# A gated linear attention kernel: per-head vector work gathered into operations over all heads, and the loop over heads put in another order

## The chip, the cores and the metric

One core of a Trainium2 chip. The metric is the device time of one execution in microseconds (us), taken as the median of several runs. The engines are TensorE (PE, whose weight loads the profile calls PEld), VectorE (DVE), ScalarE (ACT), GpSimd (POOL) and SyncE (SP), which issues the DMAs here. All data is float32 unless said otherwise.

## The reference

Two stages stand one behind the other. The first is a gated linear attention with a complex decay, over 4 batches, 8 heads, 768 steps and a head dimension of 48; the second sends each of the 3072 rows of 384 numbers through the one expert of eight that its gate picks.

```python
mag = sqrt(a_re**2 + a_im**2); scale = minimum(mag, 0.999) / (mag + 1e-6)
a = (a_re + 1j * a_im) * scale                     # one factor per batch, head, step and row of the state
for t in range(768):
    S = a[:, :, t, :, None] * S                    # state 48 x 48 per batch and head
    S.re += einsum('bhd,bhe->bhde', k[:, :, t], v[:, :, t])
    y[:, :, t] = einsum('bhd,bhde->bhe', q[:, :, t], S.re)
x = y.transpose(0, 2, 1, 3).reshape(3072, 384)
...                                                # gate: logits, argmax, softmax weight
out[mask] = gate_w[mask, None] * (maximum(x[mask] @ w1[e], 0) @ w2[e])   # for each expert e
```

## The kernel before, in words

The attention runs in six chunks (loop over `c`) of L = 128 steps, for all BH = 32 pairs of batch and head together. The states `S0r` and `S0i` stay in SBUF from chunk to chunk. A chunk has four parts:

- **Loads** (`load_t`, lines 159 to 166). v comes in four DMAs. a_re and a_im come pair by pair: a DMA into `raw` (two buffers), a transpose on PE into a PSUM tile `tp`, and a copy on DVE into `are` or `aim`, which hold 48 partitions x 4096 elements.
- **Scan** (lines 173 to 211). DVE scales the factors and forms running complex products over the 128 steps in seven doubling steps, on whole 48 x 4096 tiles. The result is `cr` and `ci`. `qc` and `kc` serve as scratch, and after seven swaps `are` and `aim` are free.
- **Loads of q and k** (lines 212 and 213) into `qc` and `kc`, by the same `load_t`.
- **Loop over the 32 heads** (lines 215 to 290). With c the running product, DVE forms Q = q c (`Qr`, `Qi`) and K = k c / |c|^2 (`Kr`, `Ki`, by way of `m2`, `t3` and a reciprocal, line 232). PE multiplies them to the 128 x 128 scores `Wt` (lines 240 and 241), DVE copies these out of PSUM, and POOL sets those above the diagonal to zero (`affine_select`, line 244). PE forms y from the scores and v and from Q and the state (lines 246, 247 and 250); DVE copies y; PE transposes it (254); DVE copies again and SP stores it into `x_attn` in DRAM. Then K is transposed (260, 264), multiplied with v (`Pr`, `Pi`, lines 268 and 270), and ten small operations on DVE (279 to 290) make the new state of the head.

All PSUM tiles of the attention (`tp`, `Wt_ps`, `y_ps`, `yT_ps`, `KrT_ps`, `KiT_ps`, `Pr_ps`, `Pi_ps`) share one tag `"r"` with four buffers. Tiles in SBUF from `pool` have two buffers, those from `big` one.

The tile framework puts in all the waits, hands out the buffers, and plans the order in which each engine gets its instructions, from the order of the source and an estimate of when each instruction can run. So the order on an engine is not always that of the source. Each engine then works through its own list in order.

The expert part (`moe_bf16`, lines 18 to 102) starts with a DMA of the whole `x_attn` into `xT` (line 32). It is not part of the change.

Of the kernel before, what the change touches and what calls it, by code (L numbers as in the profile page):

```python
# [10 lines left out]
F32 = mybir.dt.float32  # L11
BF16 = mybir.dt.bfloat16
AX = mybir.AxisListType
Alu = mybir.AluOpType
# [91 lines left out]
def kernel(  # L106
# [14 lines left out]
    nc = tc.nc  # L121
    B, H, S, D = q.shape
    BH = B * H
    L = 128
# [12 lines left out]
    ppool = ctx.enter_context(tc.psum_pool(name="ps", bufs=2))  # L137
# [4 lines left out]
    ident = cpool.tile([128, 128], F32, name="ident")  # L142
# [8 lines left out]
    for c in range(NC):  # L151
# [59 lines left out]
        cr, ci = cs, ci_s  # L211
        load_t(qc, q)
        load_t(kc, k)

        for bh in range(BH):
            b = bh // H
            h = bh % H
            crb = cr[:, b, h, :]
            cib = ci[:, b, h, :]
            qb = qc[:, b, h, :]  # L220
            kb = kc[:, b, h, :]
            vb = vc[:, b, h, :]
            Qr = pool.tile([D, L], F32, name="Qr")
            Qi = pool.tile([D, L], F32, name="Qi")
            nc.vector.tensor_tensor(Qr[:], qb, crb, Alu.mult)
            nc.vector.tensor_tensor(Qi[:], qb, cib, Alu.mult)
            m2 = pool.tile([D, L], F32, name="m2")
            t3 = pool.tile([D, L], F32, name="t3")
            nc.vector.tensor_tensor(m2[:], crb, crb, Alu.mult)
            nc.vector.tensor_tensor(t3[:], cib, cib, Alu.mult)  # L230
            nc.vector.tensor_tensor(m2[:], m2[:], t3[:], Alu.add)
            nc.vector.reciprocal(m2[:], m2[:])  # L232
            Kr = pool.tile([D, L], F32, name="Kr")
            Ki = pool.tile([D, L], F32, name="Ki")
            nc.vector.tensor_tensor(Kr[:], kb, crb, Alu.mult)
            nc.vector.tensor_tensor(Kr[:], Kr[:], m2[:], Alu.mult)  # L236
            nc.vector.tensor_tensor(Ki[:], kb, cib, Alu.mult)
            nc.vector.tensor_tensor(Ki[:], Ki[:], m2[:], Alu.mult)  # L238
            Wt_ps = ppool.tile([L, L], F32, name="Wt_ps", tag="r", bufs=4)
            nc.tensor.matmul(Wt_ps[:], Kr[:], Qr[:], start=True, stop=False)  # L240
            nc.tensor.matmul(Wt_ps[:], Ki[:], Qi[:], start=False, stop=True)  # L241
# [3 lines left out]
            y_ps = ppool.tile([L, D], F32, name="y_ps", tag="r", bufs=4)  # L245
            nc.tensor.matmul(y_ps[:], Wt[:], vb, start=True, stop=False)  # L246
            nc.tensor.matmul(y_ps[:], Qr[:], S0r[bh][:], start=False, stop=False)  # L247
# [143 lines left out]
```

## Time and profile before

| what | value |
|---|---|
| time, median of 4 runs | 4247.18 us (4245.32 to 4248.85) |
| the profiled execution | 4248.85 us, its span 4247.1 us |
| busy share of the span | PE 39%, PEld 23%, DVE 72%, ACT 1%, POOL 2% |
| granted TensorE clock | 1.000 |
| instructions on DVE | 7480 |
| chain that ended last, by engine | DVE 47%, PE 31%, DMA 15%, issue 4%, POOL 2%, ACT 1% |

The busy share is a mean over the span; the six chunks and the expert part behind them have different limits. The chain is followed back from the last instruction, at each step to what released it. The first chunk's scan ends at 299 us, its q and k loads at 367 us, its heads at 613 us; the last chunk's heads end at 3649 us.

### The profile page before, as it was taken

What the parts mean: (1) busy time and instruction counts of PE and PEld (TensorE: products, weight loads), DVE (VectorE), ACT (ScalarE), POOL (GpSimd) and SP (SyncE); (2) the same over time, 40 slices, a digit from 0 to 9 for tenths busy, and PEclk for the clock granted to TensorE, in tenths of its full rate; (3) what the DMA queues carried; (4) which work ended last, traced back from release to release, by engine and by line L of the source; (5) the groups of instructions that cost most, each with busy time, mean ns of one, the idle gap of its engine ahead of it and who ended that gap; (6) DMA issues with size and microseconds to landing.
All of it is one profiled execution on the core that took longest, in us unless ns stands there. A gap on an engine that the chain in (4) does not pass through costs nothing.

```text
span 4247.1 us, 25082 instructions
## 1 busy us (share of the span) xinstructions
PE 1676.0 (39%) x6864; PEld 971.9 (23%) x6864; DVE 3067.5 (72%) x7480; ACT 29.1 (1%) x32; POOL 83.0 (2%) x199
## 2 busy tenths in 40 slices
PE   2005541015540025530045520055410155599999
PEld 0003430003420014310024300034200043444444
DVE  4995756976748957749957659867579667777776
ACT  0000000000000000000000000000000000000000
POOL 0000000000000000000000000000000000000000
PEclk9999999999999999999999999999999999999999
DMA  1000000000010000010000000000000000401001
GB/s 24 0 4 13 4 15 12 0 10 8 3 20 6 0 14 4 4 24 0 0 16 4 12 15 0 7 10 3 17 9 0 13 5 4 165 30 60 30 1 45
DMA packets 167213, 64.62 MB, mean 15 GB/s; under 512 B 143138, under 2 KB 163618, under 8 KB 166690
## 3 DMA queue, kind: packets, MB, share of 16 engines
q1 hardware_dynamic: 167074, 63.02, 6.0%
q8 instruction: 56, 0.92, 0.1%
q14 instruction: 83, 0.68, 0.1%
HBM read 53.51 MB, written 9.44 MB: 15 GB/s over the span
## 4 chain that ended last, share of the span: by engine, by line
DVE 47%; PE 31%; DMA 15%; issue 4%; POOL 2%; ACT 1%; SPq 0%; DVEq 0%; POOLq 0%; ACTq 0%
PE z_ps L97 6%; PE hT_ps L93 5%; DMA raw<-in_a_re_dram 4%; DMA raw<-in_a_im_dram 4%; DVE qc L203 4%; DVE kc L204 4%; DVE kc L201 4%; DVE qc L200 4%; DVE cr L185 4%; DVE m L232 4%; PE tp L165 3%; DMA raw<-in_k_dram 3%; PE Wt_ps L240 3%; PE y_ps L246 3%; DMA raw<-in_q_dram 3%
## 5 line engine op out<-in xcount | busy, mean ns | idle before, releaser
L165 PE MATMUL tp<-ident,raw 128*48 128x128 f32 x768 | 288.4, 381 | 1894.5 <-DVE qc L166 1300.3
L165 PEld LDWEIGHTS tp<-ident,raw 128*48 128x48 f32 x768 | 88.2, 116 | 2093.4 <-DVE qc L166 1402.9
L95 DVE TENSOR_SCALAR hT<-hT_ps 128x512 bf16<-128x512 f32 x384 | 254.4, 689 | 137.5 <-PE hT_ps L93 120.2
L97 PE MATMUL z_ps<-w2e,hT 128*128 128x384 bf16 x1536 | 287.5, 328 | 9.2 <-DVE hT L95 7.6
L240 PE MATMUL Wt_ps<-Qr,Kr 48*128 48x128 f32 x384 | 152.0, 498 | 347.1 <-DVE Kr L236 347.1
L93 PE MATMUL hT_ps<-xTb,w1e 128*128 128x512 bf16 x1152 | 285.5, 381 | 0.1
L252 DVE COPY y_sb<-y_ps 128x48 f32<-128x48 f32 x192 | 39.9, 208 | 266.4 <-PE y_ps L250 265.5
L246 PE MATMUL y_ps<-vc,Wt 128*128 128x48 f32 x384 | 126.8, 430 | 183.1 <-POOL Wt L244 183.1
L166 DVE COPY are<-tp 48x128 f32<-48x128 f32 x192 | 53.8, 283 | 177.7 <-PE tp L165 176.8
L240 PEld LDWEIGHTS Wt_ps<-Qr,Kr 48*128 48x128 f32 x384 | 95.5, 307 | 377.1 <-DVE Kr L236 374.1
L232 DVE RECIPROCAL m<-m 48x128 f32<-48x128 f32 x192 | 179.3, 934 | 0.2
L97 PEld LDWEIGHTS <-hT 128*128 128x128 bf16 x1536 | 123.4, 97 | 176.8 <-DVE hT L95 122.7
L185 DVE RECIPROCAL cr<-cr 48x4096 f32<-48x4096 f32 x6 | 154.5, 25745 | 0.2
L166 DVE COPY aim<-tp 48x128 f32<-48x128 f32 x192 | 52.5, 282 | 138.2 <-PE tp L165 137.2
L244 POOL TENSOR_SCALAR_AFFINE_SELECT Wt<-Wt 128x128 f32<-128x128 f32 x192 | 82.0, 427 | 3547.4 <-DVE Wt L243 3547.4
L166 DVE COPY kc<-tp 48x128 f32<-48x128 f32 x192 | 52.9, 278 | 136.2 <-PE tp L165 135.7
L246 PEld LDWEIGHTS y_ps<-vc,Wt 128*128 128x128 f32 x384 | 95.9, 310 | 239.6 <-POOL Wt L244 239.6
L241 PE MATMUL Wt_ps<-Qi,Ki 48*128 48x128 f32 x384 | 140.7, 469 | 5.8 <-DVE Ki L238 5.8
L93 PEld LDWEIGHTS <-w1e 128*128 128x128 bf16 x1152 | 113.3, 98 | 118.1 <-issue 2.1
L166 DVE COPY qc<-tp 48x128 f32<-48x128 f32 x192 | 50.5, 277 | 108.4 <-PE tp L165 108.1
L247 PE MATMUL y_ps<-S0rA,Qr 48*128 48x48 f32 x384 | 126.8, 428 | 0.0
L250 PE MATMUL y_ps<-S0iA,negQi 48*128 48x48 f32 x384 | 119.7, 410 | 0.0
(2005 smaller groups left out, 3551.1 us busy)
## 6 DMA issues: line engine op xcount, KB each, us to landing
w1f<-in_moe_w_dram SPq DMA_DIRECT2D x8, 1536.0 KB, 6.5
w2f<-in_moe_w_dram SPq DMA_DIRECT2D x8, 1536.0 KB, 8.0
vc<-in_v_dram SPq DMA_DIRECT2D x24, 192.0 KB, 3.8
raw<-in_a_re_dram SPq DMA_DIRECT2D x192, 24.0 KB, 1.7
raw<-in_a_im_dram SPq DMA_DIRECT2D x192, 24.0 KB, 1.7
raw<-in_q_dram SPq DMA_DIRECT2D x192, 24.0 KB, 1.7
raw<-in_k_dram SPq DMA_DIRECT2D x192, 24.0 KB, 1.7
x_attn<-yT_sb SPq DMA_DIRECT2D x192, 24.0 KB, 1.4
```

The lines of the kernel that those rows point to most:

```text
L93: nc.tensor.matmul(hT_ps[:], w1e[:, dc, fc * 128:(fc + 1) * 128], xTb[:, dc, t0:t0 + TTK], start=(dc == 0), stop=(dc == nDC - 1))
L95: nc.vector.tensor_relu(hT[:], hT_ps[:])
L97: nc.tensor.matmul(z_ps[z][:], hT[:, z * nT:(z + 1) * nT], w2e[:, fc, :], start=(fc == 0), stop=(fc == nF - 1))
L165: nc.tensor.transpose(tp[:], raw[:], ident[:L, :L])
L166: nc.vector.tensor_copy(dst[:, b_, h_, :], tp[:])
L185: nc.vector.reciprocal(tmp[:], tmp[:])
L200: nc.vector.tensor_tensor(tA[:, :, :, :n_], a_hi, a_lo, Alu.mult)
L201: nc.vector.tensor_tensor(tB[:, :, :, :n_], b_hi, b_lo, Alu.mult)
L203: nc.vector.tensor_tensor(tA[:, :, :, :n_], a_hi, b_lo, Alu.mult)
L232: nc.vector.reciprocal(m2[:], m2[:])
L240: nc.tensor.matmul(Wt_ps[:], Kr[:], Qr[:], start=True, stop=False)
L246: nc.tensor.matmul(y_ps[:], Wt[:], vb, start=True, stop=False)
```

## The change

Per-head operations on DVE become operations over all heads. Q (`arf`, `aif`, in place of `are` and `aim`), the squared magnitude and its reciprocal (`m2a`, the reciprocal in 16 slices of 256 elements), and minus the imaginary part of Q (`t3a`) are formed once per chunk on 48 x 4096 tiles, ahead of the loop over heads. K is formed in place in `cr` and `ci` by `group_K`, in four operations of 48 x 512 for a group of four heads: the first group ahead of the loop, each later group in the loop over the group before it, one operation in each head. `crL` and `ciL` keep the last step of the running product, since `cr` and `ci` are overwritten.

The loop over heads has a new order: the scores of the head (`head_W`), the transpose and the store of y of the head before (`head_yT`), one operation of `group_K`, the transposes of K, then y, then `Pr` and `Pi`, which are kept for all heads in `Pr_all` and `Pi_all`. Behind the loop the states of all heads are updated together, by 14 operations of 48 x 1536. The matmuls, the transposes, the DMAs and the seven copies out of PSUM per head are as many as before.

```diff
--- before.py
+++ after.py
@@ -209,85 +209,117 @@
             ci_s, cid = cid, ci_s
             d_ *= 2
         cr, ci = cs, ci_s
+        crL = pool.tile([D, BH, 1], F32, name="crL")
+        ciL = pool.tile([D, BH, 1], F32, name="ciL")
+        nc.vector.tensor_copy(crL[:], cr[:, :, :, L - 1:L].rearrange("d b h l -> d (b h) l"))
+        nc.vector.tensor_copy(ciL[:], ci[:, :, :, L - 1:L].rearrange("d b h l -> d (b h) l"))
         load_t(qc, q)
         load_t(kc, k)
-
-        for bh in range(BH):
+        crf = cr.rearrange("d b h l -> d (b h l)")
+        cif = ci.rearrange("d b h l -> d (b h l)")
+        qf = qc.rearrange("d b h l -> d (b h l)")
+        kf = kc.rearrange("d b h l -> d (b h l)")
+        arf = are.rearrange("d b h l -> d (b h l)")
+        aif = aim.rearrange("d b h l -> d (b h l)")
+        nc.vector.tensor_tensor(arf[:], qf[:], crf[:], Alu.mult)
+        nc.vector.tensor_tensor(aif[:], qf[:], cif[:], Alu.mult)
+        Qr_all, Qi_all = are, aim
+        m2a = pool.tile([D, BH * L], F32, name="m2a", bufs=1)
+        t3a = pool.tile([D, BH * L], F32, name="t3a", bufs=1)
+        nc.vector.tensor_tensor(m2a[:], crf[:], crf[:], Alu.mult)
+        nc.vector.tensor_tensor(t3a[:], cif[:], cif[:], Alu.mult)
+        nc.vector.tensor_tensor(m2a[:], m2a[:], t3a[:], Alu.add)
+        for i_ in range(16):
+            w_ = BH * L // 16
+            nc.vector.reciprocal(m2a[:, i_ * w_:(i_ + 1) * w_], m2a[:, i_ * w_:(i_ + 1) * w_])
+        negQi_all = t3a.rearrange("d (b h l) -> d b h l", b=B, h=H)
+        nc.vector.tensor_scalar(t3a[:], aif[:], -1.0, None, Alu.mult)
+        Kr_all, Ki_all = cr, ci
+        GW = 4 * L
+
+        def group_K(g, i_):
+            s_ = slice(g * GW, (g + 1) * GW)
+            dst = crf if i_ < 2 else cif
+            nc.vector.tensor_tensor(dst[:, s_], dst[:, s_], (kf if i_ % 2 == 0 else m2a)[:, s_], Alu.mult)
+
+        for i_ in range(4):
+            group_K(0, i_)
+        Pr_all = pool.tile([D, BH, D], F32, name="Pr_all", bufs=1)
+        Pi_all = pool.tile([D, BH, D], F32, name="Pi_all", bufs=1)
+
+        def head_W(bh):
             b = bh // H
             h = bh % H
-            crb = cr[:, b, h, :]
-            cib = ci[:, b, h, :]
-            qb = qc[:, b, h, :]
-            kb = kc[:, b, h, :]
-            vb = vc[:, b, h, :]
-            Qr = pool.tile([D, L], F32, name="Qr")
-            Qi = pool.tile([D, L], F32, name="Qi")
-            nc.vector.tensor_tensor(Qr[:], qb, crb, Alu.mult)
-            nc.vector.tensor_tensor(Qi[:], qb, cib, Alu.mult)
-            m2 = pool.tile([D, L], F32, name="m2")
-            t3 = pool.tile([D, L], F32, name="t3")
-            nc.vector.tensor_tensor(m2[:], crb, crb, Alu.mult)
-            nc.vector.tensor_tensor(t3[:], cib, cib, Alu.mult)
-            nc.vector.tensor_tensor(m2[:], m2[:], t3[:], Alu.add)
-            nc.vector.reciprocal(m2[:], m2[:])
-            Kr = pool.tile([D, L], F32, name="Kr")
-            Ki = pool.tile([D, L], F32, name="Ki")
-            nc.vector.tensor_tensor(Kr[:], kb, crb, Alu.mult)
-            nc.vector.tensor_tensor(Kr[:], Kr[:], m2[:], Alu.mult)
-            nc.vector.tensor_tensor(Ki[:], kb, cib, Alu.mult)
-            nc.vector.tensor_tensor(Ki[:], Ki[:], m2[:], Alu.mult)
             Wt_ps = ppool.tile([L, L], F32, name="Wt_ps", tag="r", bufs=4)
-            nc.tensor.matmul(Wt_ps[:], Kr[:], Qr[:], start=True, stop=False)
-            nc.tensor.matmul(Wt_ps[:], Ki[:], Qi[:], start=False, stop=True)
+            nc.tensor.matmul(Wt_ps[:], Kr_all[:, b, h, :], Qr_all[:, b, h, :], start=True, stop=False)
+            nc.tensor.matmul(Wt_ps[:], Ki_all[:, b, h, :], Qi_all[:, b, h, :], start=False, stop=True)
             Wt = pool.tile([L, L], F32, name="Wt")
             nc.vector.tensor_copy(Wt[:], Wt_ps[:])
             nc.gpsimd.affine_select(Wt[:], Wt[:], pattern=[[1, L]], compare_op=Alu.is_ge, fill=0.0, base=0, channel_multiplier=-1)
-            y_ps = ppool.tile([L, D], F32, name="y_ps", tag="r", bufs=4)
-            nc.tensor.matmul(y_ps[:], Wt[:], vb, start=True, stop=False)
-            nc.tensor.matmul(y_ps[:], Qr[:], S0r[bh][:], start=False, stop=False)
-            negQi = pool.tile([D, L], F32, name="negQi")
-            nc.vector.tensor_scalar(negQi[:], Qi[:], -1.0, None, Alu.mult)
-            nc.tensor.matmul(y_ps[:], negQi[:], S0i[bh][:], start=False, stop=True)
-            y_sb = pool.tile([L, D], F32, name="y_sb")
-            nc.vector.tensor_copy(y_sb[:], y_ps[:])
+            return Wt
+
+        def head_yT(bh, y_sb):
+            b = bh // H
+            h = bh % H
             yT_ps = ppool.tile([D, L], F32, name="yT_ps", tag="r", bufs=4)
             nc.tensor.transpose(yT_ps[:], y_sb[:], ident[:L, :L])
             yT_sb = pool.tile([D, L], F32, name="yT_sb")
             nc.vector.tensor_copy(yT_sb[:], yT_ps[:])
             nc.sync.dma_start(out=x_dram[h * D:(h + 1) * D, b * S + t0:b * S + t0 + L], in_=yT_sb[:])
 
+        y_prev = None
+        for bh in range(BH):
+            b = bh // H
+            h = bh % H
+            vb = vc[:, b, h, :]
+            Wt = head_W(bh)
+            if y_prev is not None:
+                head_yT(bh - 1, y_prev)
+            if bh // 4 + 1 < BH // 4:
+                group_K(bh // 4 + 1, bh % 4)
             KrT_ps = ppool.tile([L, D], F32, name="KrT_ps", tag="r", bufs=4)
-            nc.tensor.transpose(KrT_ps[:], Kr[:], ident[:D, :D])
+            nc.tensor.transpose(KrT_ps[:], Kr_all[:, b, h, :], ident[:D, :D])
             KrT = pool.tile([L, D], F32, name="KrT")
             nc.vector.tensor_copy(KrT[:], KrT_ps[:])
             KiT_ps = ppool.tile([L, D], F32, name="KiT_ps", tag="r", bufs=4)
-            nc.tensor.transpose(KiT_ps[:], Ki[:], ident[:D, :D])
+            nc.tensor.transpose(KiT_ps[:], Ki_all[:, b, h, :], ident[:D, :D])
             KiT = pool.tile([L, D], F32, name="KiT")
             nc.vector.tensor_copy(KiT[:], KiT_ps[:])
+            y_ps = ppool.tile([L, D], F32, name="y_ps", tag="r", bufs=4)
+            nc.tensor.matmul(y_ps[:], Wt[:], vb, start=True, stop=False)
+            nc.tensor.matmul(y_ps[:], Qr_all[:, b, h, :], S0r[bh][:], start=False, stop=False)
+            nc.tensor.matmul(y_ps[:], negQi_all[:, b, h, :], S0i[bh][:], start=False, stop=True)
+            y_sb = pool.tile([L, D], F32, name="y_sb")
+            nc.vector.tensor_copy(y_sb[:], y_ps[:])
+            y_prev = y_sb
             Pr_ps = ppool.tile([D, D], F32, name="Pr_ps", tag="r", bufs=4)
             nc.tensor.matmul(Pr_ps[:], KrT[:], vb, start=True, stop=True)
             Pi_ps = ppool.tile([D, D], F32, name="Pi_ps", tag="r", bufs=4)
             nc.tensor.matmul(Pi_ps[:], KiT[:], vb, start=True, stop=True)
-            Pr = pool.tile([D, D], F32, name="Pr")
-            Pi = pool.tile([D, D], F32, name="Pi")
-            nc.vector.tensor_copy(Pr[:], Pr_ps[:])
-            nc.vector.tensor_copy(Pi[:], Pi_ps[:])
-            crL = crb[:, L - 1:L]
-            ciL = cib[:, L - 1:L]
-            a_ = pool.tile([D, D], F32, name="a_")
-            b_ = pool.tile([D, D], F32, name="b_")
-            nc.vector.tensor_scalar(a_[:], Pi[:], ciL, None, Alu.mult)
-            nc.vector.scalar_tensor_tensor(a_[:], Pr[:], crL, a_[:], Alu.mult, Alu.add)
-            nc.vector.tensor_scalar(b_[:], S0i[bh][:], ciL, None, Alu.mult)
-            nc.vector.scalar_tensor_tensor(b_[:], S0r[bh][:], crL, b_[:], Alu.mult, Alu.subtract)
-            c_ = pool.tile([D, D], F32, name="c_")
-            d_ = pool.tile([D, D], F32, name="d_")
-            nc.vector.tensor_scalar(c_[:], Pi[:], crL, None, Alu.mult)
-            nc.vector.scalar_tensor_tensor(c_[:], Pr[:], ciL, c_[:], Alu.mult, Alu.subtract)
-            nc.vector.tensor_scalar(d_[:], S0r[bh][:], ciL, None, Alu.mult)
-            nc.vector.scalar_tensor_tensor(d_[:], S0i[bh][:], crL, d_[:], Alu.mult, Alu.add)
-            nc.vector.tensor_tensor(S0r[bh][:], a_[:], b_[:], Alu.add)
-            nc.vector.tensor_tensor(S0i[bh][:], c_[:], d_[:], Alu.add)
+            nc.vector.tensor_copy(Pr_all[:, bh, :], Pr_ps[:])
+            nc.vector.tensor_copy(Pi_all[:, bh, :], Pi_ps[:])
+        head_yT(BH - 1, y_prev)
+
+        crLb = crL.broadcast_to([D, BH, D])
+        ciLb = ciL.broadcast_to([D, BH, D])
+        tA2 = pool.tile([D, BH, D], F32, name="tA2", bufs=1)
+        tB2 = pool.tile([D, BH, D], F32, name="tB2", bufs=1)
+        nc.vector.tensor_tensor(tA2[:], Pr_all[:], crLb, Alu.mult)
+        nc.vector.tensor_tensor(tB2[:], Pi_all[:], ciLb, Alu.mult)
+        nc.vector.tensor_tensor(tA2[:], tA2[:], tB2[:], Alu.add)
+        nc.vector.tensor_tensor(tB2[:], S0iA[:], ciLb, Alu.mult)
+        tC2 = pool.tile([D, BH, D], F32, name="tC2", bufs=1)
+        nc.vector.tensor_tensor(tC2[:], S0rA[:], crLb, Alu.mult)
+        nc.vector.tensor_tensor(tC2[:], tC2[:], tB2[:], Alu.subtract)
+        nc.vector.tensor_tensor(tB2[:], S0iA[:], crLb, Alu.mult)
+        tD2 = pool.tile([D, BH, D], F32, name="tD2", bufs=1)
+        nc.vector.tensor_tensor(tD2[:], S0rA[:], ciLb, Alu.mult)
+        nc.vector.tensor_tensor(tD2[:], tD2[:], tB2[:], Alu.add)
+        nc.vector.tensor_tensor(tB2[:], Pi_all[:], crLb, Alu.mult)
+        nc.vector.tensor_tensor(Pr_all[:], Pr_all[:], ciLb, Alu.mult)
+        nc.vector.tensor_tensor(tB2[:], Pr_all[:], tB2[:], Alu.subtract)
+        nc.vector.tensor_tensor(S0rA[:], tA2[:], tC2[:], Alu.add)
+        nc.vector.tensor_tensor(S0iA[:], tB2[:], tD2[:], Alu.add)
 
     gstack.close()
     if True:
```

## Rows read from the trace of the kernel before

**Rows 1.** The page, part 1: busy us (share of span) and instructions, per engine.
```profile
PE 1676.0 (39%) x6864; PEld 971.9 (23%) x6864; DVE 3067.5 (72%) x7480; ACT 29.1 (1%) x32; POOL 83.0 (2%) x199
```

**Rows 2.** Busy time by stretch (start:end, length, busy of each engine, clock, DMA).
```profile
366.90:372.36 5.46, 4.21 (x18) 3.15 (x17) 2.21 (x11) 0.00 (x0) 0.29 (x1) 1.00 0.05 11
...
453.62:461.61 7.99, 4.35 (x17) 3.22 (x18) 5.80 (x29) 0.00 (x0) 0.46 (x1) 1.00 0.01 3
...
366.95:612.60 245.65, 139.56 (x547) 102.81 (x546) 175.65 (x859) 0.00 (x0) 13.75 (x32) 1.00 0.02 4
299.40:366.95 67.55, 22.42 (x60) 6.93 (x61) 26.70 (x102) 0.00 (x0) 0.00 (x0) 1.00 0.12 22
```

**Rows 3.** Timeline, a steady head: start, us, engine, line, out<-in, [idle before <-releaser].
```profile
455.42 0.46 POOL L244 TENSOR_SCALAR_AFFINE_SELECT Wt<-Wt 128x128 f32<-128x128 f32 x1 [7.53 <-DVE Wt L243]
...
455.65 0.37 DVE L226 TENSOR_TENSOR Qi<-qc,ci 48x128 f32<-48x128 f32 x1
...
455.94 0.66 PE L246 MATMUL y_ps<-vc,Wt 128*128 128x48 f32 x2 [0.98 <-POOL Wt L244]
...
457.65 0.21 DVE L252 COPY y_sb<-y_ps 128x48 f32<-128x48 f32 x1 [1.43 <-PE y_ps L250]
...
461.61 0.79 PE L240 MATMUL Wt_ps<-Qr,Kr 48*128 48x128 f32 x2 [2.16 <-DVE Kr L236]
```

**Rows 4.** Timeline of PE and POOL, the chunk's second head.
```profile
374.05 0.29 POOL L244 TENSOR_SCALAR_AFFINE_SELECT Wt<-Wt 128x128 f32<-128x128 f32 x1 [5.18 <-DVE Wt L243]
...
374.40 0.67 PE L246 MATMUL y_ps<-vc,Wt 128*128 128x48 f32 x2 [0.81 <-POOL Wt L244]
...
375.45 0.62 PE L250 MATMUL y_ps<-S0iA,negQi 48*128 48x48 f32 x2
...
376.38 0.41 PE L254 MATMUL yT_ps<-ident,y_sb 128*48 128x128 f32 x1 [0.30 <-DVE y_sb L252]
...
376.72 0.34 PE L260 MATMUL KrT_ps<-ident,Kr 48*128 48x48 f32 x1
...
376.86 0.30 PE L264 MATMUL KiT_ps<-ident,Ki 48*128 48x48 f32 x1
...
377.36 0.40 PE L268 MATMUL Pr_ps<-vc,KrT 128*48 128x48 f32 x2 [0.19 <-DVE KrT L262]
...
377.84 0.79 PE L240 MATMUL Wt_ps<-Qr,Kr 48*128 48x128 f32 x2
...
378.43 0.63 PE L241 MATMUL Wt_ps<-Qi,Ki 48*128 48x128 f32 x2
```

**Rows 5.** Groups of instructions on DVE by shape: busy us, mean ns | idle before.
```profile
L232 DVE RECIPROCAL m<-m 48x128 f32<-48x128 f32 x192 | 179.3, 934 | 0.2
L185 DVE RECIPROCAL cr<-cr 48x4096 f32<-48x4096 f32 x6 | 154.5, 25745 | 0.2
...
L179 DVE TENSOR_TENSOR cr<-are 48x4096 f32<-48x4096 f32 x6 | 26.5, 4416 | 0.2
...
L183 DVE TENSOR_SCALAR ci<-cr 48x4096 f32<-48x4096 f32 x6 | 13.7, 2285 | 22.1 <-ACT cr L182 22.1
...
L200 DVE TENSOR_TENSOR qc<-are 48x2048 f32<-48x2048 f32 x6 | 13.7, 2276 | 0.0
```

**Rows 6.** Groups on DVE in 904 to 974, the second chunk's q and k loads.
```profile
L166 DVE COPY kc<-tp 48x128 f32<-48x128 f32 x32 | 8.8, 278 | 22.5 <-PE tp L165 22.5
L166 DVE COPY qc<-tp 48x128 f32<-48x128 f32 x32 | 8.4, 277 | 18.2 <-PE tp L165 18.1
```

**Rows 7.** Timeline of DVE, from one chunk to the next.
```profile
611.07 0.20 DVE L274 COPY Pi<-Pi_ps 48x48 f32<-48x48 f32 x1
...
612.40 0.19 DVE L290 TENSOR_TENSOR S0iA<-c__2927,d__2928 48x48 f32<-48x48 f32 x1
...
617.87 0.56 DVE L166 COPY are<-tp 48x128 f32<-48x128 f32 x2 [5.08 <-PE tp L165]
```

**Rows 8.** Timeline of DVE behind the last chunk.
```profile
3663.75 4.96 DVE L34 CAST xTb<-xT 128x9216 bf16<-128x9216 f32 x1 [4.43 <-DMA xT<-x_attn]
```

## The prediction

> **What bounds the kernel now.** I read the page first: VectorE (DVE) is busy 72% of the span, TensorE (PE) 39% [rows 1]. That is a mean over stages, so next come the windows, for one chunk: loading q and k takes 67.55 us, of which DVE works 26.70; the loop over heads takes 245.65 us, DVE 175.65, PE 139.56 [rows 2]. Neither engine is full in the heads, so a chain sets the pace. A steady head is 7.99 us (PE 4.35, DVE 5.80); one of the first four, whose inputs DVE had prepared during the loads, is 5.46 (PE 4.21) [rows 2]; 28 x 7.99 + 4 x 5.46 = 245.6. The timeline gives the chain: PE waits 2.16 for Kr before the next score product, then 0.98 for the mask on POOL before y, and DVE waits 1.43 for y before it copies it [rows 3]. In the quick heads the first wait is gone, and 0.81 (mask), 0.30 (y copied) and 0.19 (KrT copied) are left [rows 4].
>
> **The loop over heads.** Per head the change takes 21 of 28 DVE instructions out and leaves seven copies, plus in 28 of the 32 heads one 48x512 product of group_K. A copy is 0.20 to 0.28 [rows 3, 6, 7], so about 1.6 us. A two-tensor operation of 2048 elements is 2.276 and of 4096 is 4.416 [rows 5], slope 1.045 ns an element; 512 elements are then 0.67 and 1536 are 1.74. DVE needs 2.3 us a head and is no bound. PE keeps all its matmuls. Their time without waits, from starts in the second head [rows 4]: y 374.40 to 376.07, 1.67; yT 0.34; KrT 0.14; KiT 0.30; Pr and Pi, 377.36 to 377.84, 0.48; the score pair, 377.84 to 379.06, 1.22. Sum 4.15, and with the three waits 5.45, which is the 5.46 measured. In the new order yT of the head before, KrT and KiT (0.78) stand between the score pair and y, so of the mask's 0.81 to 0.98 only 0.03 to 0.20 is left; yT no longer waits, as its y is copied during the next score pair, and Pr doesn't, as KrT is copied during y. That makes 4.18 to 4.35. I take 4.3: 32 x 4.3 = 137.6, a gain of 108.05 a chunk. Below, 4.15 (no wait at all); above, 5.46, should the waits stay as in the quick heads.
>
> Behind the waiting y on PE stand Pr, Pi and the next score pair; behind the waiting y copy on DVE the Pr and Pi copies. Nothing else hangs on them, and the 192 stores on SP are the same.
>
> **The batch ahead of the heads.** New on DVE, per chunk: three 48x4096 products for m2a (13.2), 16 reciprocals of 256 elements (between 0.934 for 128 and 25.745 for 4096 the slope is 6.25 ns, so 1.73 each, 27.7), two products with q (8.8), the negation (2.3, as the tensor_scalar of that size), group_K of the first four heads (2.7) [rows 5]; the two small copies of the last column are under 0.5. Sum 54.8. Before, the reciprocals alone were 32 x 0.934 = 29.9, so they are no saving to speak of; where the work lies is what counts. m2a and the reciprocals need only the scan, and can lie beside the loads. There DVE idles 18.2 + 22.5 = 40.7 us before the copies [rows 6], and of its 26.70 [rows 2] 9.5 are no copies (8.8 + 8.4 are) but preparation of four heads that the change removes. So 50.2 are free for 54.8: 4.6 over. A 4.4 us product also holds up the copies behind it. Four PSUM banks and two raw tiles let six loads run ahead, at 67.55 / 64 = 1.06 us a load; I allow two such products, 8.8, for what doesn't fit. That is 13 us more a chunk. Bounds: 0 if all fits; 54.8 - 9.5 = 45.3 if none does.
>
> The cover is an order of DVE instructions that the framework plans; line 226 of the next head standing behind line 244 of this one [rows 3] shows that it does move work into gaps. If its idea of a load or a reciprocal is far off, the cover is lost.
>
> **The state update behind the heads.** Fourteen 48x1536 operations replace ten 48x48 ones a head. tC2 and tD2's first products need no Pr and can go into gaps in the heads; twelve remain behind the last Pi copy, 12 x 1.74 = 20.9, where before 1.5 us stood (611.07 to 612.59) [rows 7]: 19.4 more in front of the next chunk's copies. DVE idled 5.08 there anyway, until the first loads behind v had landed [rows 7], and six loads run ahead (6.4 us). That leaves 8. Bounds: 2, if copies slip in between the operations; 19.4, if none of it is covered. are and aim are now held until the last head's y, but their reload had followed the heads before, too; this costs nothing as long as that order holds, and one load's 1.06 otherwise. Behind the last chunk DVE idled 4.43 for xT [rows 8], so 15 of the 19.4 show: 7 more than in the others.
>
> **Sum.** -108.05 + 13 + 8 = -87.05 a chunk, x 6 = -522, + 7 = -515. The profiled execution takes 4248.85, 0.04% above the median of the runs, 4247.18; so 3733. The scan, and the expert part behind the chunks, are not touched.
>
> **The rivals.**
>
> *Quick-head pace.* The planner orders PE so that the waits stay: 32 x 5.46 = 174.7 instead of 137.6, +37.1 a chunk, 3956. For it: the first four heads had their inputs ready and still ran so [rows 4]. Against: there yT stood directly behind its own y, which the new source undoes. 0.10.
>
> *The batch is not hidden.* +45.3 instead of +13 a chunk, x 6 = +194: 3927. For it: an in-order queue, long instructions. Against: DVE already fills the load gaps with 9.5 us of such work. 0.11.
>
> *All of it is hidden.* 4.15 a head (-4.8), loads +0 (-13), update +2 (-6): -23.8 x 6 = -143: 3590. For it: the window has nearly the room; against: the sum exceeds the room by 4.6. 0.08.
>
> *POOL and DVE block each other.* The mask takes 0.29 beside an idle DVE [rows 4] and 0.46 where line 226 ran beside it, which itself took 0.37 where 128 elements cost 0.28 otherwise [rows 3]. So they do disturb each other, by 0.17. Were a mask held for a whole 48x512 product in each of the 28 heads that has one, 28 x 0.67 = 18.8 a chunk, +113: 3846. Against: in the source's order the product starts behind the yT copy, when the mask has begun. 0.05. The Trainium skill, "SBUF — State Buffer", section "SBUF: two separate sides", states that of a VectorE operation with two SBUF inputs and a GpSimd operation, whichever starts first holds the shared port pair for its whole instruction and the other fully blocks. By that rule the wait could be a whole product, which is this rival; the 0.17 in the trace is less than the 0.28 of a product, so the trace shows a delay but not that size.
>
> *Slower.* Seven tiles per head go through four PSUM banks, each freed by a DVE copy. If the new order made PE wait for banks behind DVE's products until a head took again what it takes now, the gain of 108 would vanish: 4248.85 + 6 x 21 + 7 = 4382. It decides from (245.65 - 21) / 32 = 7.0 us a head, 2.7 above my pace, four waits of a whole 0.67 product in each head. Against: before, the same seven tiles share the four banks, and the waits of PE are for data [rows 3, 4]. 0.03. That gain and cost cancel, as though the planner had restored the old order: 0.01.
>
> **How the numbers follow.** The forecast as summed has 0.62, with a range of its own from 3640 to 3830 (pace 4.15 to 4.6, loads +5 to +25). The range of 3590 to 3930 leaves out about half of "all hidden" (0.04), most of the quick-head pace (0.08), half of "not hidden" (0.05) and the last two (0.04): 0.2. About 0.2% is what a measurement of this kernel can tell from no change. Faster by more: 0.96; within: 0.01; slower: 0.03.
>
> **What the profile after would show.** Heads: windows of some 138 us with PE busy nearly throughout, DVE about half; y's wait for POOL under 0.2 and yT without one. Loads: DVE busy 60 us or more of some 80, and reciprocals between the q and k copies; a row of reciprocals without copies while PE waits for DVE would be the second rival. Behind the heads: some 21 us of 48x1536 operations, PE waiting for the copies of are. Expert part: as before. The prediction is wrong if the heads stay above 5 us, if the loads grow by more than 25, or if the planner puts batch work in front of the heads' copies.

## The result, and the profile after

| what | before | after |
|---|---|---|
| time, median | 4246.24 us (13 runs) | 3653.98 us (9 runs, 3652.60 to 3656.25) |
| ratio, 95% interval | | 0.8605 [0.8597, 0.8614] |
| span of the profiled execution | 4247.1 us | 3652.5 us |
| granted TensorE clock | 1.000 | 1.000 |
| instructions on DVE | 7480 | 3868 |

The change takes 592 us off by the medians, 595 by the profiled spans, where 515 were forecast. One of the 13 runs before took 4372.48 us and lies apart; the other twelve took 4243.31 to 4249.75. The page's part 1 of the kernel after, beside [rows 1]: PE has as many instructions as before, DVE half as many, and DVE's busy time is a tenth less.

```profile
PE 1616.1 (44%) x6864; PEld 959.3 (26%) x6864; DVE 2751.8 (75%) x3868; ACT 29.1 (1%) x32; POOL 57.0 (2%) x199
```

Windows of the fourth chunk after, with the columns of [rows 2]: loads, heads, the stretch behind the last `Pi` copy, and one head.

```profile
1828.20:1896.84 68.64, 22.60 (x61) 6.91 (x61) 68.62 (x102) 0.00 (x0) 0.00 (x0) 1.00 0.12 21
1896.84:2029.35 132.51, 128.63 (x545) 100.76 (x545) 56.84 (x242) 0.00 (x0) 9.35 (x32) 1.00 0.03 7
2029.35:2051.11 21.76, 3.88 (x11) 1.13 (x11) 21.62 (x22) 0.00 (x0) 0.00 (x0) 1.00 0.27 49
1900.96:1905.09 4.13, 4.03 (x18) 3.15 (x17) 2.02 (x9) 0.00 (x0) 0.29 (x1) 1.00 0.02 6
```

Each stage now has one full engine: DVE in the loads (68.62 of 68.64 us, 26.70 of 67.55 before) and behind the heads (21.62 of 21.76), PE in the heads (128.63 of 132.51). A full engine need not be what sets a stage's length; for the loads the experiments ask that.

The head of the last window in the timeline; the columns are those of [rows 3].

```profile
1900.96 0.79 PE L254 MATMUL Wt_ps<-are,cr 48*128 48x128 f32 x2
...
1902.12 0.41 PE L265 MATMUL yT_ps<-ident,y_sb 128*48 128x128 f32 x1
...
1902.45 0.34 PE L281 MATMUL KrT_ps<-ident,cr 48*128 48x48 f32 x1
...
1902.65 0.29 POOL L258 TENSOR_SCALAR_AFFINE_SELECT Wt<-Wt 128x128 f32<-128x128 f32 x1 [3.83 <-DVE Wt L257]
...
1903.00 0.66 PE L289 MATMUL y_ps<-vc,Wt 128*128 128x48 f32 x2
1903.07 0.67 DVE L243 TENSOR_TENSOR ci<-ci,kc 48x512 f32<-48x512 f32 x1
...
1904.61 0.39 PE L296 MATMUL Pr_ps<-vc,KrT 128*48 128x48 f32 x2
```

No matmul of this head carries a wait any more. The mask (line 258) falls under the three transposes, and y starts 0.06 behind its end, where PE waited 0.81 to 0.98 before [rows 3, 4]. From start to start the score pair takes 1.16, yT 0.33, KrT and KiT with the gap for the mask 0.55, y 1.61, Pr and Pi 0.48: 4.13.

Timeline of DVE at the end of the scan; lines 229 to 231 form `m2a`, line 205 is the scan's last operation, and line 312 is an operation of the state update that needs no `Pr`.

```profile
1821.68 4.41 DVE L229 TENSOR_TENSOR m2a<-cr 48x4096 f32<-48x4096 f32 x1
1826.01 2.28 DVE L205 TENSOR_TENSOR ci<-qc,kc 48x2048 f32<-48x2048 f32 x1
1828.21 1.75 DVE L312 TENSOR_TENSOR tC<-S0rA,crL 48x1536 f32<-48x1536 f32 x1
...
1829.99 1.27 DVE L166 COPY qc<-tp 48x128 f32<-48x128 f32 x6
1831.19 4.41 DVE L230 TENSOR_TENSOR t3a<-ci 48x4096 f32<-48x4096 f32 x1
1835.52 0.87 DVE L166 COPY qc<-tp 48x128 f32<-48x128 f32 x4
```

The planner of the tile framework put line 229 ahead of the scan's last operation, where no load covers it (4.33 us from start to start), and line 312 ahead of the first copy of q. In the loads behind that, each long product is followed by four or five copies back to back: loads had gone on landing while it ran.

Groups on DVE in that chunk's loads, beside [rows 6]: the idle time before the copies, 18.2 and 22.5 us before, is gone.

```profile
L234 DVE RECIPROCAL m2a<-m2a 48x256 f32<-48x256 f32 x16 | 27.6, 1729 | 0.0
L166 DVE COPY kc<-tp 48x128 f32<-48x128 f32 x30 | 6.9, 262 | 0.0
L166 DVE COPY qc<-tp 48x128 f32<-48x128 f32 x32 | 6.7, 257 | 0.0
```

Timeline of DVE behind the heads, beside [rows 7], and at the end behind the last chunk, beside [rows 8].

```profile
2029.90 1.74 DVE L307 TENSOR_TENSOR tA<-Pr_all,crL 48x1536 f32<-48x1536 f32 x1
...
2036.57 0.28 DVE L166 COPY are<-tp 48x128 f32<-48x128 f32 x1
...
2049.44 1.74 DVE L322 TENSOR_TENSOR S0iA<-tB,tD 48x1536 f32<-48x1536 f32 x1
2051.11 1.07 DVE L166 COPY are<-tp 48x128 f32<-48x128 f32 x5
...
3075.49 1.70 DVE L82 CAST w1e<-w1f 128x3072 bf16<-128x3072 f32 x1
...
3082.10 4.96 DVE L34 CAST xTb<-xT 128x9216 bf16<-128x9216 f32 x1
```

Twelve operations of the state update stand there, 1.67 us from start to start when nothing lies between, with six copies of the next chunk's `are` slipped in and five waiting behind. Behind the last chunk the cast of `xT` waits no more; casts of weights have moved ahead of it.

Three marks cut a chunk in the same way in both traces: start of the scan's last operation (line 205), first score matmul, last `Pi` copy. Means over the chunks:

| stretch of a chunk, us | before | after | difference |
|---|---|---|---|
| last scan operation to first score (loads) | 69.7 | 71.2 | +1.5 |
| first score to last `Pi` copy (heads) | 244.3 | 132.5 | -111.8 |
| last `Pi` copy to the next mark (update, loads of v and a, scan) | 293.4 | 304.2 | +10.8 |
| the same, last chunk, to the end of the span | 599.5 | 608.1 | +8.6 |

Of the 10.8, 4.3 is line 229, which belongs to the batch. So by these marks the batch costs 5.8 a chunk and the update 6.5. Over the kernel: 6 x (-111.8 + 5.8) + 5 x 6.5 + 8.6 = -595, the difference of the two spans. The marks put line 312 to the batch, though it belongs to the update: the run without the update, below, has 70.5 in the loads, so 0.7 of the 1.5 is the update's, and the two cost 5.1 and 7.2.

### The profile page after: what moved, and what is told of

Its sections match the earlier page's. It is cut to its first block, busy times and chain, and to the rows that moved or that the text cites. A ratio compares the mean times of both kernels' runs of the same rounds, so it can differ in the third digit from the quotient of the medians.

```text
span 3652.5 us, 21614 instructions
## 1 busy us (share of the span) xinstructions
PE 1616.1 (44%) x6864; PEld 959.3 (26%) x6864; DVE 2751.8 (75%) x3868; ACT 29.1 (1%) x32; POOL 57.0 (2%) x199
## 4 chain that ended last, share of the span: by engine, by line
DVE 53%; PE 33%; DMA 9%; issue 3%; POOL 2%; ACT 1%; DVEq 0%; POOLq 0%; ACTq 0%
PE z_ps L97 7%; PE hT_ps L93 6%; DVE qc L203 4%; DVE kc L204 4%; DVE kc L201 4%; DVE qc L200 4%; DVE cr L185 4%; DMA raw<-in_a_im_dram 4%; PE Wt_ps L254 4%; DVE m2a L234 4%; PE y_ps L289 3%; PE y_ps L290 3%; DMA raw<-in_a_re_dram 3%; DVE ci L205 2%; DVE cr L202 2%
## 5 line engine op out<-in xcount | busy, mean ns | idle before, releaser
L257 DVE COPY Wt<-Wt_ps 128x128 f32<-128x128 f32 x192 | 55.9, 291 | 190.9 <-PE Wt_ps L255 186.4
L97 PEld LDWEIGHTS <-hT 128*128 128x128 bf16 x1536 | 122.2, 97 | 177.6 <-DVE hT L95 127.0
L234 DVE RECIPROCAL m2a<-m2a 48x256 f32<-48x256 f32 x96 | 165.7, 1731 | 0.0
L254 PE MATMUL Wt_ps<-are,cr 48*128 48x128 f32 x384 | 152.3, 498 | 0.0
L290 PE MATMUL y_ps<-S0rA,are 48*128 48x48 f32 x384 | 126.8, 429 | 0.0
L255 PE MATMUL Wt_ps<-aim,ci 48*128 48x128 f32 x384 | 121.1, 417 | 0.0
L291 PE MATMUL y_ps<-S0iA,t3a 48*128 48x48 f32 x384 | 119.7, 410 | 0.0
L100 DVE SCALAR_TENSOR_TENSOR out_acc<-z_ps,sc_all,out_acc 128x384 f32<-128x384 f32 x192 | 105.2, 610 | 18.3 <-PE z_ps L97 18.3
L255 PEld LDWEIGHTS Wt_ps<-aim,ci 48*128 48x128 f32 x384 | 104.3, 330 | 0.0
L291 PEld LDWEIGHTS y_ps<-S0iA,t3a 48*128 48x128 f32 x384 | 104.3, 330 | 0.0
```

The lines of the kernel that those rows point to most:

```text
L97: nc.tensor.matmul(z_ps[z][:], hT[:, z * nT:(z + 1) * nT], w2e[:, fc, :], start=(fc == 0), stop=(fc == nF - 1))
L234: nc.vector.reciprocal(m2a[:, i_ * w_:(i_ + 1) * w_], m2a[:, i_ * w_:(i_ + 1) * w_])
L254: nc.tensor.matmul(Wt_ps[:], Kr_all[:, b, h, :], Qr_all[:, b, h, :], start=True, stop=False)
L255: nc.tensor.matmul(Wt_ps[:], Ki_all[:, b, h, :], Qi_all[:, b, h, :], start=False, stop=True)
L290: nc.tensor.matmul(y_ps[:], Qr_all[:, b, h, :], S0r[bh][:], start=False, stop=False)
L291: nc.tensor.matmul(y_ps[:], negQi_all[:, b, h, :], S0i[bh][:], start=False, stop=True)
```

## The experiments

The theory is that of the prediction: DVE is off the path of the heads because of the batch, PE's waits are gone because of the order, and the batch is hidden in the loads because DVE idles there. Ratios are to the kernel before.

**The batch without the order.** The kernel after, y and its transpose back in their old places.

```diff
             Wt = head_W(bh)
-            if y_prev is not None:
-                head_yT(bh - 1, y_prev)
             if bh // 4 + 1 < BH // 4:
                 group_K(bh // 4 + 1, bh % 4)
+            y_ps = ppool.tile([L, D], F32, name="y_ps", tag="r", bufs=4)
...
+            nc.vector.tensor_copy(y_sb[:], y_ps[:])
+            head_yT(bh, y_sb)
...
             nc.vector.tensor_copy(KiT[:], KiT_ps[:])
-            y_ps = ppool.tile([L, D], F32, name="y_ps", tag="r", bufs=4)
...
-            y_prev = y_sb
```

> The changed kernel with its vector work batched, but the loop over heads in the order of before: scores, y, transpose and store of y, transposes of K, Pr and Pi, all of the same head. Theory: the batch takes the preparation off the chain, but the waits for the mask, for y and for KrT stay, so a head takes 5.46 us, as the first four heads of the kernel before, instead of 4.13 in the changed one: 32 x 1.33 = 42.6 a chunk, x 6 = 255, so about 3910 us. Rival: the order is worth nothing once DVE is relieved; heads stay at 4.13 and the time at 3654.

3927.37 us, 0.9236 [0.9222, 0.9250]: the theory. The timeline of one head:

```profile
431.30 0.79 PE L254 MATMUL Wt_ps<-are,cr 48*128 48x128 f32 x2
...
433.33 0.66 PE L278 MATMUL y_ps<-vc,Wt 128*128 128x48 f32 x2 [0.81 <-POOL Wt L258]
...
435.31 0.41 PE L265 MATMUL yT_ps<-ident,y_sb 128*48 128x128 f32 x1 [0.30 <-DVE y_sb L282]
...
436.29 0.40 PE L293 MATMUL Pr_ps<-vc,KrT 128*48 128x48 f32 x2 [0.20 <-DVE KrT L287]
...
436.78 0.79 PE L254 MATMUL Wt_ps<-are,cr 48*128 48x128 f32 x2
```

These are the three waits of the quick heads [rows 4]: 5.48 from score to score. Most heads have that pace, but 177.6 a chunk is 5.55 a head. In 24 of the 192 heads a product of `group_K` runs into the mask, as here (timeline of DVE and POOL):

```profile
382.32 0.67 DVE L243 TENSOR_TENSOR cr<-cr,m2a 48x512 f32<-48x512 f32 x1
382.47 0.68 POOL L258 TENSOR_SCALAR_AFFINE_SELECT Wt<-Wt 128x128 f32<-128x128 f32 x1 [5.12 <-DVE Wt L257]
```

The mask takes 0.68 us there, once 1.28, where it takes 0.29 alone: some 10 us in the whole kernel. The batch alone gives 319 us; the order, on top of it, 273.

**The order without the batch.** The kernel before with only y, yT and the `head_yT` of the head before moved as in the change.

```diff
+            if y_prev is not None:
+                head_yT(bh - 1, y_prev)
             KrT_ps = ppool.tile([L, D], F32, name="KrT_ps", tag="r", bufs=4)
...
             nc.vector.tensor_copy(KiT[:], KiT_ps[:])
+            y_ps = ppool.tile([L, D], F32, name="y_ps", tag="r", bufs=4)
...
+            y_prev = y_sb
```

> The kernel before with only the new order in the loop over heads: y of the head before is transposed behind the scores of this one, the transposes of K stand ahead of y; all vector work stays per head. Theory: the chain is gone but DVE now binds, with the 5.80 us that it is busy per head of before; heads take 5.9 to 6.2 us, some 193 a chunk instead of 244, so about 3940 us. Rival 1: the order alone brings the pace of the changed kernel, 4.13 us a head; then, with the loads of before and no update behind the heads, about 3575. Rival 2: the order does nothing without the batch, 4246.

4155.18 us, 0.9772 [0.9757, 0.9787]: between the theory and no gain at all, so the theory's number failed. Timeline of PE:

```profile
502.60 0.79 PE L250 MATMUL Wt_ps<-Qr,Kr 48*128 48x128 f32 x2 [2.60 <-DVE Kr L246]
...
510.58 0.79 PE L250 MATMUL Wt_ps<-Qr,Kr 48*128 48x128 f32 x2 [3.79 <-DVE Kr L246]
...
517.38 0.79 PE L250 MATMUL Wt_ps<-Qr,Kr 48*128 48x128 f32 x2 [2.60 <-DVE Kr L246]
```

The waits inside the head are gone, but PE now waits 2.60 and 3.79 in turn for the next head's `Kr`. DVE's list has that head's preparation, in one head all of it and in the next the part from the reciprocal on, behind this head's `Pi` copy, and DVE idles 1.2 to 1.4 for y before it. The order is worth 91 us alone, since DVE's work for the next head sits in the chain.

**The order, with the preparation written ahead of y.** This asks whether DVE's work or only its place held that kernel up.

```diff
+        nxt = prep(0)
         for bh in range(BH):
...
+            crb, cib, vb, Qr, Qi, Kr, Ki, negQi = nxt
...
             nc.vector.tensor_copy(KiT[:], KiT_ps[:])
+            if bh + 1 < BH:
+                nxt = prep(bh + 1)
             y_ps = ppool.tile([L, D], F32, name="y_ps", tag="r", bufs=4)
```

> The kernel before with the new order, as in the run with the order alone (4155), and the per-head preparation of Q and K for the next head put ahead of this head's copy of y; no batch. Theory: the order alone gained little because the preparation stood on DVE's list behind this head's Pi copy, so that PE's next scores waited 2.6 to 3.8 us for Kr behind it; with the preparation ahead, DVE is full: its 28 instructions need some 5.5 to 5.8 us a head, 176 to 186 a chunk instead of 227.7, so 3845 to 3905. Rival 1: the place does nothing, DVE's instructions a head are too many in any order: 4155. Rival 2: with the chain gone a head takes PE's 4.13 even without the batch: about 3580.

3779.87 us, 0.8898 [0.8883, 0.8913]: faster than the range expected, and still 126 us slower than the change. Timeline of one head, and its window with the columns of [rows 2]:

```profile
474.45 0.79 PE L259 MATMUL Wt_ps<-Qr,Kr 48*128 48x128 f32 x2 [0.49 <-DVE Kr L245]
...
477.13 0.66 PE L277 MATMUL y_ps<-vc,Wt 128*128 128x48 f32 x2 [0.74 <-POOL Wt L263]
...
477.47 0.27 DVE L238 TENSOR_TENSOR m<-cr 48x128 f32<-48x128 f32 x1
477.67 0.27 DVE L239 TENSOR_TENSOR t<-ci 48x128 f32<-48x128 f32 x1
...
479.78 0.79 PE L259 MATMUL Wt_ps<-Qr,Kr 48*128 48x128 f32 x2 [0.49 <-DVE Kr L245]
```

```profile
474.45:479.78 5.33, 4.10 (x17) 3.15 (x17) 5.33 (x29) 0.00 (x0) 0.29 (x1) 1.00 0.02 5
```

A head takes 5.33 and DVE has no idle time in it: it is the bound. The expectation summed durations; two such products start 0.20 apart, not 0.27. The first three heads of a chunk, for which most of the preparation was done during the loads, take 4.13, the pace of the change, without any batch. So the new order with the preparation in its new place takes the heads from 244.3 to 166.4 us a chunk, which is the 466 us of this kernel, and the relief of DVE takes them from there to 132.5: 33.9 x 6 = 203. The change pays for that relief with its dearer loads and update, about 13 a chunk against this kernel, and 126 are left.

**The batch without its reciprocals.**

```diff
-        for i_ in range(16):
-            w_ = BH * L // 16
-            nc.vector.reciprocal(m2a[:, i_ * w_:(i_ + 1) * w_], m2a[:, i_ * w_:(i_ + 1) * w_])
```

> The changed kernel without the 16 reciprocals (K is multiplied with the squared magnitude itself). They are 27.7 us of DVE a chunk. Theory: the batch lies beside the loads of q and k, which have a pace of their own of about 67.5 us and are stretched by it by only some 5; without the reciprocals the time falls by 5 to 6 us a chunk, to about 3620. Rival: DVE's work sets the loads' length outright, and all 27.7 come off: 3654 - 166 = 3488.

3656.16 us, 0.8597 [0.8583, 0.8612], no different from the change: theory and rival both missed. The window of the loads and the copies' group in them:

```profile
1828.20:1899.00 70.80, 22.48 (x60) 6.96 (x60) 56.85 (x101) 0.00 (x0) 0.00 (x0) 1.00 0.12 20
...
L166 DVE COPY qc<-tp 48x128 f32<-48x128 f32 x32 | 8.0, 279 | 12.7 <-PE tp L165 12.3
```

DVE, with 14 us of idle time again, is no faster through the stage. So although it is full in the change, it is not what sets the stage's length: the loads are. The chain of waits of the kernel after runs over DVE's work for most of the stage, since there DVE and the loads need nearly the same time; at the end of the stage it shows the cycle of the loads: start, length, what.

```profile
1892.33 0.39 PE tp L165
...
1892.74 1.54 DMA raw<-in_k_dram
1894.28 0.14 issue
1894.42 0.39 PE tp L165
```

A transfer, its transpose, then the next transfer into the same buffer: 2.09 us from one to the next, with two buffers of `raw` 1.05 a load, 67 us for 64 loads.

**One reciprocal of 4096 elements in place of 16.**

```diff
-        for i_ in range(16):
-            w_ = BH * L // 16
-            nc.vector.reciprocal(m2a[:, i_ * w_:(i_ + 1) * w_], m2a[:, i_ * w_:(i_ + 1) * w_])
+        nc.vector.reciprocal(m2a[:], m2a[:])
```

> The changed kernel with one reciprocal of 4096 elements (25.7 us) in place of the 16 slices. Theory: what matters is not the sum of DVE's work beside the loads but how long a copy out of PSUM stands behind one instruction. Four PSUM banks and two raw tiles let six loads run ahead, 6.4 us at 1.06 us a load, so 25.7 - 6.4 = 19 us a chunk show: about 3654 + 116 = 3770. Rival: only the sum counts, and it is the same: 3654.

3781.46 us, 0.8900 [0.8887, 0.8912]: the theory. The timeline of DVE shows why the same work costs 127 us, 21 a chunk, in one piece:

```profile
316.18 0.87 DVE L166 COPY qc<-tp 48x128 f32<-48x128 f32 x4
316.98 25.73 DVE L232 RECIPROCAL m2a<-m2a 48x4096 f32<-48x4096 f32 x1
342.64 1.22 DVE L166 COPY qc<-tp 48x128 f32<-48x128 f32 x6
```

Six copies wait behind it, so six loads had run ahead; four PSUM buffers and two `raw` tiles hold no more. Six loads are 6.4 us, so 19 of the 25.7 us should be lost to the loads, and 21 were. A slice of 1.73 or a product of 4.41 is less than the six loads, 6.4.

**The kernel after without the state update**, which the last two parts of the prediction price.

```diff
...
-        nc.vector.tensor_tensor(tA2[:], Pr_all[:], crLb, Alu.mult)
...
-        nc.vector.tensor_tensor(S0iA[:], tB2[:], tD2[:], Alu.add)
```

> The changed kernel without the update of the states behind the heads (14 operations of 48x1536 a chunk left out; the states stay zero). Theory: of the 20 us that stand behind a chunk's heads some 6 show between chunks and some 9 ahead of the expert part, plus the 1.7 of tC2 in front of the q copies: 5 x 6.4 + 9 + 6 x 1.7 = 51, so about 3603. Rival 1: all of it shows, 6 x 22 = 132: 3522. Rival 2: the first loads of the next chunk cover it all: 3654.

3606.49 us, 0.8482 [0.8469, 0.8494]: the theory. 47.5 us for the update of six chunks, where the twelve operations behind the heads alone are 12 x 1.74 x 6 = 125 on DVE. By the marks it is 6.4 behind the heads, 10.1 behind the last chunk's, and 0.7 in each chunk's loads (line 312).

**No update behind the last chunk**, whose state nobody reads.

```diff
+        if c < NC - 1:
+            crLb = crL.broadcast_to([D, BH, D])
...
```

> The changed kernel without the update of the states behind the last chunk, which nothing reads. Theory: the load of xT waits for the last of these operations (it starts 0.2 us behind it), but casts of the first expert weights have moved ahead of it; the stretch from the last Pi copy to the end is 608.1 us now and was 599.4 before, so about 9 us come off: 3645. Rival 1: all 20 come off: 3634. Rival 2: none, 3654.

3646.13 us, 0.8580 [0.8568, 0.8592]: the theory, 7.9 us.

**The update in groups of eight heads**, inside the loop, none in the last chunk. `update` holds the same 14 operations, on 48x384 elements each; GH is 8.

```diff
+            if (bh + 1) % GH == 0 and c < NC - 1:
+                update(bh + 1 - GH)
```

> The changed kernel with the update of the states in four groups of eight heads, each behind its heads (operations of 48x384, 0.5 us each), and none in the last chunk. Theory: DVE is busy 57 of the 132 us of the heads, so three of the four groups fit there at no cost; what stands behind the heads falls from 20 us to some 6 and is hidden by the wait for v. With the last chunk's 9: 3654 - 5 x 6.4 - 9 = 3613. Rival: the 48x384 operations hold up copies that PE waits for, up to 0.5 us each for 42 of them, and the heads lose up to 20 us a chunk: 3650 to 3745.

3629.82 us, 0.8541 [0.8529, 0.8553], between theory and rival. What follows the heads falls by 6 to 298.2 us a chunk, as expected, but the heads grow from 132.5 to 136.9 in the five chunks with an update. Timeline of DVE, POOL and PE where a group's update stands:

```profile
2428.04 0.54 DVE L281 TENSOR_TENSOR tB<-S0iA,ciL 48x384 f32<-48x384 f32 x1
...
2428.18 0.55 POOL L258 TENSOR_SCALAR_AFFINE_SELECT Wt<-Wt 128x128 f32<-128x128 f32 x1 [4.59 <-DVE Wt L257]
...
2428.79 0.66 PE L314 MATMUL y_ps<-vc,Wt 128*128 128x48 f32 x2 [1.12 <-POOL Wt L258]
```

The planner put a group's twelve operations into one head and the start of the next (2425.97 to 2432.5) and the head's copies between them; PE waits 1.12 for the mask. Fifteen heads, three a chunk, take 5.5 so. This is the prediction's last condition for being wrong, batch work in front of the heads' copies, made true by hand, for 4.4 us a chunk.

**The two squares of `m2a` on ScalarE.**

```diff
-        nc.vector.tensor_tensor(m2a[:], crf[:], crf[:], Alu.mult)
-        nc.vector.tensor_tensor(t3a[:], cif[:], cif[:], Alu.mult)
+        nc.scalar.activation(m2a[:], crf[:], Act.Square)
+        nc.scalar.activation(t3a[:], cif[:], Act.Square)
```

> The changed kernel with the two squares of m2a on ScalarE, which is idle there. In the changed kernel the planner has put the first of them, 4.4 us, ahead of the last operation of the scan, on which the loads of q wait. Theory: this is what the batch costs, as the reciprocals cost nothing; without it the loads of q start 4.4 us earlier in each chunk: 3654 - 26 = 3628. Rival 1: the loads' end is set by DVE's sum, and then both squares come off, 8.8 a chunk: 3601. Rival 2: nothing changes, 3654.

3629.94 us, 0.8544 [0.8532, 0.8555]: the theory. Of two products moved, only the one that stood ahead of the scan's last operation pays: 24 us are 4.0 a chunk. The loads stay at 72.0, and what follows the heads falls from 304.2 to 300.1.

**Six buffers for the loads, after and before.** The loads' pace, by the theory that came out of the missing reciprocals, is two buffers' doing; and the cover of the batch with it. The same edit goes into both kernels.

```diff
-                raw = pool.tile([L, D], F32, name="raw", tag="raw")
+                raw = pool.tile([L, D], F32, name="raw", tag="raw", bufs=6)
```

> The changed kernel with six buffers instead of two for the raw tiles of the loads. Theory: the loads have a pace of 1.06 us because only two are in flight; with six they run at 0.4 to 0.5. The loads of a then shrink by some 30 us a chunk (the update in front of them stays); those of q and k hardly, since DVE is busy 68.62 of 68.64 us there: only group_K's operations, 10 us, can move into the heads. About 39 a chunk, 3420. Rival 1: the reciprocals are no bound as their removal showed, so the loads of q and k shrink like the others: 65 a chunk, 3264. Rival 2: another resource sets the pace of the loads, 3654.

> The kernel before with six buffers instead of two for the raw tiles. Theory: nothing much lies beside its loads (DVE 27 of 67.6 us beside those of q and k), so all four shrink to about half, 72 us a chunk: 4247 - 430 = 3817. The change is then worth about 400 us instead of 593, as the loads that hid its batch are no longer there. Rival: the loads shrink alike in both kernels and the change is worth 593 still: if this takes 3817, the changed kernel takes 3224.

3426.15 us, 0.8063 [0.8050, 0.8077], for the kernel after, the theory; 3788.05 us, 0.8915 [0.8902, 0.8929], for the kernel before, faster than expected by 29. The copies of the first chunk's `are`, when DVE has nothing else to do, give the pace: durations, then first and last start, of the kernel before and of the kernel after with six buffers. Of the latter there are also three rows of the timeline.

```profile
L166 DVE COPY are<-tp x32: 282/282/284, 9.0 to 43.1; 48x128 f32<-48x128 f32 x32
```

```profile
L166 DVE COPY are<-tp x32: 282/283/283, 8.8 to 23.0; 48x128 f32<-48x128 f32 x32
...
8.80 12.21 SPq L163 DMA_DIRECT2D raw<-in_a_re_dram  x26
...
279.69 2.13 DVE L166 COPY qc<-tp 48x128 f32<-48x128 f32 x10
...
303.83 21.07 DVE L234 RECIPROCAL m2a<-m2a 48x256 f32<-48x256 f32 x13
```

1.10 us a load (34.1 / 31) becomes 0.46. With six tiles SP issues 26 loads in a row, 0.47 us from one to the next, so by then SP's issuing sets the pace rather than the tiles; no run with more tiles tests this. In the loads of q, ten copies now stand behind a long product instead of four or five: six `raw` tiles and four PSUM buffers are ten. By the three marks, six buffers take the kernel before from 69.7 to 31.7 us in the loads of q and k and from 293.4 to 254.6 behind the heads, where v and a are loaded. The kernel after goes from 71.2 to 66.1 and from 304.2 to 272.6. In its loads of q and k DVE now sets the length: the timeline shows thirteen reciprocals in a row behind the last copy. The heads stay as they were, 244.3 and 132.5. So with six buffers the change gains the same 111.8 in the heads but pays 34.4 + 4.3 for the batch instead of 5.8, and 13.7 for the update instead of 6.5 (line 312 once more counted to the batch): 59.4 a chunk, 356 us, by the times 362, where it was 592.

**Three edits together:** six buffers, squares on ScalarE, update by eight and none in the last chunk.

> The changed kernel with six raw buffers, the squares of m2a on ScalarE, and the state update in groups of eight heads, none in the last chunk. Theory: what these brought by themselves adds up, and the squares now count both, since DVE binds beside the loads of q and k: 3420 (six buffers) - 16 - 9 - 6 x 8.8 = about 3340. Rival: the update by eight costs more in the heads and the loads are bound by DMA again, no better than six buffers alone: 3420.

3332.34 us, 0.7842 [0.7830, 0.7854]: the theory, and the fastest of all, 322 us below the kernel after. Its heads take 138.8 us with the update in them and 132.8 in the last chunk, without.

## Why the prediction was right

The forecast was 3733, its own range 3640 to 3830, and 3654 came out: the mechanism held in every stage, and each term was sized too dear. The four misses have the same sign, so they add up, to 80 us.

- **Heads**, -108.05 forecast, -111.8 measured. The pace is 4.13, not 4.3; the lower bound of 4.15 was the better value. I had kept up to 0.20 of the mask's wait and allowed for others; 0.06 was left. Undoing the order brought back 5.48, undoing the batch a wait of 2.60 to 3.79 for `Kr`. With the two undone in this way the whole is more than the sum of the parts (91 + 319 of 592). But the batch is not the only way to get the preparation out of the chain: written ahead of y, without a batch, it gave 466 of the 592. What only the relief of DVE gave is the step from 166.4 to 132.5 a chunk, 203 us in all, of which 126 are left once the dearer loads and the update are paid for. The prediction did not price the two apart.
- **The batch ahead of the heads**, +13 forecast, +5.8 measured (5.1 without line 312): the largest miss, 43 of the 80 us between forecast and result. The term that was sized wrong is "I allow two such products, 8.8, for what doesn't fit", on top of the 4.6 of its sum. The prediction's own figures speak against it: six loads run ahead, 6.4 us, which is more than a product of 4.4. Copies held up behind a product were made up for at once, and 1.5 us is all that the stage grew. What the batch did cost, 4.3, is the product that the planner put ahead of the scan's last operation, which the prediction did not foresee; so what nearness there is in this term is partly luck. The reason given, free DVE time during the loads, is right; the missing reciprocals show that one should have asked what sets the loads' time too, and six buffers that it is the number of `raw` tiles.
- **State update**, +8 forecast, +6.5 measured (7.2 with line 312 in the loads): six copies slipped in, which was the lower bound's case in part.
- **Last chunk**, +15 forecast, +8.6 measured (7.9 by leaving it out). Casts of weights and small operations filled the wait for `xT`, which I had counted as covering 4.43 only.
- **Durations** worked out from [rows 5] as 0.67 (48x512), 1.74 (48x1536) and 1.73 (reciprocal of 256) came out as 0.67, 1.74 and 1.729.
- **Rivals.** "All of it is hidden", 3590, came 64 us below the result, nearer than the forecast's 79 above it: it was right on the heads (4.15) and wrong on the batch and the update, which show with 5.8 and 6.5 where it had 0 and 2. The quick-head pace is what the batch gives without the order (5.48). The batch that isn't hidden needs faster loads or a longer instruction, and both were seen. The lock of POOL and DVE cost the change next to nothing: its masks take 0.292 us throughout, and in the 7 of 192 heads where a product starts while the mask runs, the product takes 0.74 instead of 0.67. In the old order with the batch it is real, some 10 us, since there products start ahead of masks. A head of 7.0, the slower rival's, was nowhere near.

## What to carry to other kernels

Take work off a loop's path in two steps, and price both: give the full engine less, and put what it must still do where the loop's chain does not wait for it; here the relief alone gave 319 us, the place alone 91 to 466, depending on whether all of the work that the chain waits for was moved, and both together 592. When work is hidden in another stage's gaps, ask what makes the gaps, since a fix of that cause (here four more buffers) takes the cover away, and the two gains don't add up. Cut long work on an engine that also empties buffers into pieces shorter than the time that those buffers bridge: here they bridge 6.4 us, with pieces of 1.73 and 4.41 the loads grew by 1.5 us a chunk, with one piece of 25.7 by 21 more.

## What the runs showed of the hardware

Small loads, 24 KB each on one queue, were limited by what is in flight: 1.10 us a load with two buffers. With six it is 0.46, close to the 0.47 us at which SP issues one load after the other.

DVE starts the next of two 48x128 products 0.20 us after the first, though each is listed with 0.27 to 0.28, and a 48x1536 one 1.67 for 1.74. A full engine is better summed by starts than by durations.

A mask on POOL that starts 0.14 us behind a 48x384 product on DVE took 0.55 us, where it takes 0.29 alone; the product kept its 0.54. A mask 0.15 behind a 48x512 product took 0.68, and the product kept its 0.67. In both cases, and where two products follow each other (1.28), the mask ends 0.15 to 0.16 behind the end of the product, however much of the product had been left. The other way round, a product that starts 0.09 behind a mask took 0.74 instead of 0.67, and the mask kept its 0.29. The Trainium skill, "SBUF — State Buffer", section "SBUF: two separate sides", says that of a VectorE operation with two SBUF inputs and a GpSimd operation that reads SBUF, the one that starts first holds the shared port pair for its whole instruction while the other blocks; these traces agree that the later one waits to the end of the earlier one, which loses nothing. Starts as listed do not tell the order within 0.03 us: in the steady heads before, line 225 is listed 0.02 to 0.03 behind the mask, kept its 0.28, and the mask ended 0.15 behind it, at 0.46.
